# A planner's filler matmuls and the spacing of indirect writes: two of its numbers changed in a fused attention and mixture-of-experts kernel

## The chip, the cores and the metric

The kernel runs on one core of one Trainium2 chip. The metric is device time in microseconds (us), shown as the median of three runs; lower is better. Beside it stands one profiled execution, whose trace is read here. The engines are PE (TensorE matmuls; PEld is its weight load), DVE (VectorE), ACT (ScalarE), POOL (GpSimd) and SP, which issues most DMAs. Every engine works through its own instructions in the order in which they were written.

## The reference

The attention output of 8 batches x 8 heads x 576 tokens x 64 is laid out as 4608 tokens of 512 numbers, and goes through a layer of 8 experts in which each token visits one expert:

```python
scores = scale * np.matmul(q, k.transpose(0, 1, 3, 2))       # window 32; heads 4 to 7 dilated by 4
scores = np.where(masks[None, :, :, :], scores, -1000000000.0)
attn = softmax(scores)                                       # with 1e-9 in the divisor
x = np.matmul(attn, v) -> (4608, 512)
logits = x @ w_gate                                          # (4608, 8)
expert_idx = np.argmax(logits, axis=1)
y[token] = gate_w * (np.maximum(x[token] @ w1[e], 0.0) @ w2[e])   # e = expert_idx[token], F = 1024
```

All of it is float32.

## The kernel before

**The attention** is cut into 32 units: a batch, a kind of mask, and two heads. A unit goes through `turn` (DVE transposes of q and k), `scores` (PE, line 595), `masked` (DVE, line 611), `lowest` (DVE, line 623), `exps` (ACT, line 629), `inverse` (DVE, lines 640 and 642), `norm` (POOL, line 646), `weights` (PE transposes in three groups of three, line 657), an eviction of each group to the tile eT (ACT or DVE, line 878), `summed` (PE, line 676, tile xo), and `put_x` (ACT or DVE, lines 687 and 689). The tile eT has one buffer, `two` (xo, lp and xrow in PSUM) one, and `misc` (the weights in PSUM and others) two.

**The route** of a batch follows its four units: `parts_of_logits` (PE, tile lp), a copy to ls, `logits` (PE, line 976), `choose` and `count` (DVE), `ranks` (PE, lines 1007 and 1010), `places_of` (DVE), `to_rows` (PE transposes, tile xrow, line 939), `rows_out` (ACT or DVE, line 950), and five indirect writes of rows to a table in DRAM, `bucket` (POOL, line 493). After batches 1, 2, 4 and 7, DVE also works out tables of which rows the next slots take.

**The experts** run in 33 slots of 128 rows: a read of rows from `bucket` (SP), a transpose (DVE, line 1407), 32 matmuls of 128x128 into `ph` (line 1415), two evictions, 8 matmuls of 128x512 into `py` (line 1431), an eviction, and an indirect write to the output (POOL, line 1456). Fourteen short blocks of 4 x 32 rows (tiles own, ph_s, py_s) stand between later slots. The last three slots come after the planned part.

**The order** of every engine is made by `Plan.write` while the kernel is being built. Each piece of work is a step with a planned duration, steps that it comes after, buffers that it takes, and a rank. The planner keeps a time at which each engine is free, takes the step with the lowest rank among those that can start soonest, and writes it down. An indirect write on POOL that follows another one is planned no sooner than `APART` after it, and `pass_time` puts `IDLE` memsets of a 128x1 tile, `still`, ahead of it (line 722). `APART` is 0.21 us for each memset.

**The fillers** are matmuls that nobody reads. Until the first expert step is written (`plan.until`), each PE step that is planned to start later than PE is free gets fillers of 0.22 planned us ahead of it (`fill`, line 714): as many whole ones as go into the wait less 0.2 us, at most 12, or two where the planner holds PE's clock to be low. A filler multiplies the tile `idle` by itself into the fourth quarter of the PSUM bank that `weights` (or `ranks`) last took, and so it carries that tile's name: `weights<-idle`, `rank<-idle`, or `unread<-idle` before there is one. It waits for what that bank waits for.

Of the kernel before, what the change touches and what calls it, by code (L numbers as in the profile page):

```python
# [63 lines left out]
STEP_W = 1.0  # L64
ROUTE = 5.0

IDLE = 7

MOVED = 3.0
MOVED_S = 1.5  # L70
# [47 lines left out]
class Plan:  # L118
# [12 lines left out]
    SLACK = 0.2  # L131
    WARM = 0.36
    MOST = 12
    WARMING = 2
    BIAS = 1.5
    COSTS = {"DVE": BIAS}

    APART = 0.21 * IDLE

# [66 lines left out]
    def write(self):  # L206
        left = list(self.steps)
        waiting = {id(s): sum(a.end is None for a in s.after) for s in left}
        needs = {}
        for s in left:  # L210
            for a in s.after:
                needs.setdefault(id(a), []).append(s)
        open_ = [s for s in left if not waiting[id(s)]]
        n = len(left)
        while open_:
            found = []
            for s in open_:
                free = [h.ring.free_at() for h in s.takes]
                if None not in free:
                    found.append(min(  # L220
                        (self.could(s, free, e) for e in s.engines),
                        key=lambda f: f[0] + s.us[f[2]] + self.COSTS.get(f[2], 0.0),
                    ))
            soon = min(f[0] for f in found) + self.SOON
            at, _, e, s = min((f for f in found if f[0] <= soon), key=lambda f: (f[1], f[0]))
            if e == "PE" and self.fill and not self.filled(s):
                idle, cold = at - self.free[e] - self.SLACK, self.slowed(at) > 1.0
                us = self.FILL * self.slowed(self.free[e])
                for _ in range(max(min(self.MOST, int(idle / us)), self.WARMING if cold else 0)):
                    self.fill()  # L230
                    self.free[e] = self.matmuls(self.free[e], self.FILL, self.FILL)
            if e == "PE":
                at = max(at, self.free[e])
                s.end = self.matmuls(at, s.us[e], s.dense, s.slow)
            else:
                s.end = at + s.us[e]
            self.free[e] = s.end
            s.on = None if s.moved else e
            if s.moved and e == "POOL" and self.last_indirect and self.APART:
                self.idle()  # L240
            if e == "POOL":
                self.last_indirect = bool(s.moved)
            if s.moved and e == "POOL":
                if at < self.wrote + self.BURST:
                    if not self.bursts or self.bursts[-1][1] < self.wrote:
                        self.bursts.append((self.wrote, 0.0))
                    self.bursts[-1] = self.bursts[-1][0], s.end + self.AFTER
                self.wrote = s.end
            if s.moved:
                lanes = self.lanes[e == "POOL"]  # L250
                t = s.end - s.dmas * self.ISSUE.get(e, 0.0)
                for _ in range(s.dmas):
                    t = max(t + self.ISSUE.get(e, 0.0), lanes.pop(0))
                    self.moving = max(self.moving, t + 0.65 * self.LANDS) + s.moved / s.dmas
                    lanes.append(self.moving + 0.35 * self.LANDS)
                self.free[e], s.end = t, lanes[-1]
            for h in s.takes:
                h.ring.holds.append(h)
            s.emit(e)
            for h in s.uses:  # L260
                h.left -= 1
                if s.end >= h.end:
                    h.end, h.on = s.end, s.on
            open_.remove(s)
            n -= 1
            for w in needs.get(id(s), ()):
                waiting[id(w)] -= 1
                if not waiting[id(w)]:
                    open_.append(w)
        assert n == 0  # L270
# [58 lines left out]
def kernel(  # L329
# [390 lines left out]
    def pass_time():  # L720
        for _ in range(IDLE):
            nc.gpsimd.memset(still, 0.0)  # L722
# [1115 lines left out]
```

## Time and profile before

| what | us |
|---|---|
| median of 3 runs (780.31 to 782.7) | 781.12 |
| profiled execution | 781.74 |
| span in the trace | 780.0 |
| PE busy in the span | 742.8 |
| DVE, ACT, POOL busy | 257.6, 265.2, 193.5 |

Around the span of the profiled execution lie 1.7 us. A row of the timeline has the start, the duration, the engine, the line, the operation and its tiles as out<-in; in square brackets is the idle time of the engine just before it and what ended that. Here "issue" is idle time in which the engine waited for nothing that the profile shows. A float32 matmul leaves two records on PE, so that x24 of a filler are 12 fillers; a transpose of `weights` or `xrow` leaves one. Neighbouring instructions of one kind are merged into a row.

### The profile page before, as it was taken

Reading aid. Unit: us, or ns where it says so; the run is one execution under the profiler, and the core shown is the slowest. Engines: PE = TensorE matmul, PEld = TensorE weight load, DVE = VectorE, ACT = ScalarE, POOL = GpSimd, SP = SyncE. Lnnn points to the kernel's source line nnn. Section 1 sums busy time; section 2 is a strip of 40 time slices with the busy share of each in tenths; the row PEclk is TensorE's granted clock in tenths of the full one; section 3 lists DMA queues with packets and bytes.
Section 4 is the critical chain, followed back from the end, with each engine's and each line's share of the span. In section 5 each row is a group of like instructions: output and inputs, shape, how many; then the busy total and the mean of one; then the engine's idle time right before and its main releaser. Section 6 shows DMA issues by size and latency. Waiting matters only on the chain.

```text
span 780.0 us, 21889 instructions
## 1 busy us (share of the span) xinstructions
PE 742.8 (95%) x8406; PEld 562.4 (72%) x8406; DVE 257.6 (33%) x718; ACT 265.2 (34%) x868; POOL 193.5 (25%) x641
## 2 busy tenths in 40 slices
PE   5879989999999999999999999999999999999996
PEld 5768878868787776776776776777776776766664
DVE  7958858678857740710000000000000000000000
ACT  2766756576747754211111111111111111111100
POOL 1314343425253434260100100211221111102101
PEclk9989999999999999999999999999999999999999
DMA  9878775969997979799629684727678166099660
GB/s 274 301 224 272 229 239 137 361 190 323 260 268 178 298 226 350 262 387 323 214 47 314 201 258 100 254 51 250 196 261 299 35 226 261 22 316 351 257 222 30
DMA packets 140399, 180.68 MB, mean 232 GB/s; under 512 B 68764, under 2 KB 90014, under 8 KB 139776
## 3 DMA queue, kind: packets, MB, share of 16 engines
q1 hardware_dynamic: 132864, 159.00, 64.1%
q0 software_dynamic: 6272, 19.43, 6.5%
q8 instruction: 68, 1.11, 0.6%
q10 hardware_dynamic: 1152, 0.78, 0.4%
q14 instruction: 43, 0.35, 0.1%
HBM read 252.03 MB, written 19.95 MB: 349 GB/s over the span
## 4 chain that ended last, share of the span: by engine, by line
PE 80%; issue 8%; DMA 6%; DVE 3%; ACT 2%; POOL 1%; SPq 0%; POOLq 0%; DVEq 0%; ACTq 0%
PE ph L1415 27%; PE py L1431 25%; PE scores L595 6%; PE xo L676 6%; PE weights L657 4%; DMA qT<-in_moe_w_dram 4%; PE py_s L1545 3%; PE ph_s L1518 3%; PE weights L714 3%; PE xrow L939 2%; PE lp L962 1%; DMA raw<-in_k_dram 1%; DMA x<-bucket 1%; PE logits L976 1%; ACT eT L878 1%
## 5 line engine op out<-in xcount | busy, mean ns | idle before, releaser
L1415 PEld LDWEIGHTS ph<-xt,w 128*128 128x128 f32 x2112 | 243.2, 192 | 15.7 <-issue 14.6
L1415 PE MATMUL ph<-xt,w 128*128 128x128 f32 x2112 | 252.5, 277 | 0.0
L1431 PE MATMUL py<-w,h 128*128 128x512 f32 x528 | 236.5, 594 | 0.6 <-ACT h L1426 0.6
L1431 PEld LDWEIGHTS py<-w,h 128*128 128x128 f32 x528 | 96.0, 190 | 101.3 <-issue 100.8
L629 ACT ACTIVATE e<-e,lo 128x96 f32<-128x96 f32 x288 | 103.5, 363 | 19.6 <-DVE lo L623 19.6
L1407 DVE STREAM_TRANSPOSE xt<-x 128x512 f32<-128x512 f32 x30 | 21.3, 711 | 243.7 <-PE ph L1415 240.4
L1456 POOL DMA_INDIRECT out_dram<-y,to x30 | 29.5, 984 | 251.7 <-ACT y L1436 249.2
L646 POOL TENSOR_TENSOR e<-e,rec 128x864 f32<-128x864 f32 x32 | 52.3, 1633 | 141.1 <-DVE rec L642 112.6
L1426 ACT ACTIVATE h<-ph 128x512 f32<-128x512 f32 x63 | 37.6, 597 | 142.6 <-PE ph L1415 141.8
L1436 ACT ACTIVATE y<-py,gt 128x512 f32<-128x512 f32 x30 | 20.6, 687 | 157.8 <-PE py L1431 150.3
L595 PE MATMUL scores<-kT,qT 32*64 32x96 f32 (+1 forms) x2160 | 56.2, 259 | 12.0 <-issue 7.4
L595 PEld LDWEIGHTS scores<-kT,qT 32*64 32x64 f32 (+1 forms) x2160 | 49.1, 139 | 18.5 <-issue 14.3
L722 POOL MEMSET still<- 128x1 f32 x504 | 51.4, 102 | 25.0
L629 ACT ACTIVATION_READ_ACCUMULATOR e<-e,lo 128x1 f32 x288 | 54.4, 189 | 0.0
L493 POOL DMA_INDIRECT bucket<-rows,idx x40 | 39.2, 980 | 60.9 <-issue 16.9
L676 PEld LDWEIGHTS xo<-eT,v 96*64 96x64 f32 x1280 | 40.9, 138 | 12.3 <-issue 4.5
L657 PE MATMUL weights<-cst,e 128*96 128x128 f32 x288 | 45.1, 282 | 4.5 <-ACT eT L878 2.1
L611 DVE SCALAR_TENSOR_TENSOR e<-scores,cst 128x384 f32<-128x384 f32 (+1 forms) x128 | 45.5, 395 | 10.0 <-PE scores L595 9.0
L676 PE MATMUL xo<-eT,v 96*64 96x64 f32 (+1 forms) x1280 | 45.9, 225 | 3.0 <-issue 2.6
L878 ACT COPY eT<-weights 96x384 f32<-96x384 f32 x88 | 39.9, 480 | 22.8 <-PE weights L657 16.1
L657 PEld LDWEIGHTS weights<-cst,e 128*96 128x96 f32 x288 | 30.2, 129 | 17.2 <-issue 6.8
L1511 DVE STREAM_TRANSPOSE own<-own 128x128 f32<-128x128 f32 x14 | 4.3, 304 | 99.3 <-DMA own<-bucket 99.3
(168 smaller groups left out, 566.5 us busy)
## 6 DMA issues: line engine op xcount, KB each, us to landing
w<-in_moe_w_dram SPq DMA_DIRECT2D x66, 2048.0 KB
raw<-in_moe_w_dram SPq DMA_DIRECT2D x42, 1024.0 KB
qT<-in_moe_w_dram SPq DMA_DIRECT2D x28, 512.0 KB
w<-in_moe_w_dram SPq DMA_DIRECT2D x8, 1024.0 KB
raw<-in_q_dram SPq DMA_DIRECT2D x14, 576.0 KB
raw<-in_k_dram SPq DMA_DIRECT2D x14, 576.0 KB
x<-bucket SPq DMA_DIRECT2D x120, 64.0 KB
v<-in_v_dram SPq DMA_DIRECT2D x7, 864.0 KB
```

The source lines that it names most:

```text
L493: nc.gpsimd.indirect_dma_start(out=bucket, out_offset=bass.IndirectOffsetOnAxis(ap=idx, axis=0), in_=rows, in_offset=None, bounds_check=NR ...
L595: nc.tensor.matmul(two[r][QB * half : QB * half + QB, KB * c : KB * c + KB], lhsT=qT[:, QB * n : QB * n + QB], rhs=kt[:, QB * n : QB * n + ...
L611: nc.vector.scalar_tensor_tensor(out=e[p, c0 : c0 + w], in0=sc[r][p, a : a + w], scalar=-SCALE, in1=m[p, a : a + w], op0=OP.mult, op1=OP.add,)
L629: nc.scalar.activation(out=ev[:, c], in_=ev[:, c], func=AF.Exp, bias=lo[:, c : c + 1], scale=-1.0, accum_out=den[:, c : c + 1],)
L646: nc.gpsimd.tensor_tensor(out=ev, in0=ev, in1=rec.unsqueeze(2).broadcast_to([128, NC, KB]), op=OP.mult)
L657: nc.tensor.transpose(tp[0:KB, c], ev[:, 3 * g + c], ident)
L676: nc.tensor.matmul(xo[DH * r : DH * r + DH, g, lo - half_s * g : hi - half_s * g], lhsT=v0[:, hd, n] if ty == 0 else v1[:, n, hd], rhs=eT[ ...
L722: nc.gpsimd.memset(still, 0.0)
L878: copier(e)(S_["eT"][:, 3 * g : 3 * g + 3], S_["w", g][0:KB, 0:3])
L1415: nc.tensor.matmul(ph[:, f % 4], lhsT=w1s[j % 2][:, c, 128 * f : 128 * f + 128], rhs=xt[:, c], start=c == 0, stop=c == 3,)
L1426: nc.scalar.activation(to, ph, AF.Relu)
L1431: nc.tensor.matmul(py, lhsT=h[:, f], rhs=w2s[j % 2][:, f], start=f == 0, stop=f == 7)
```

## The change

Two numbers. `IDLE` goes from 7 to 10, so that ten memsets stand between two indirect writes where seven did, and `APART` in the planner follows it (1.47 to 2.1 us). And a wait of PE that is planned to be no longer than 0.9 us beyond the 0.2 us of slack gets no fillers any more, save the two that are written where the planner holds the clock to be low.

```diff
-IDLE = 7
+IDLE = 10
...
+
+    SHORT_WAIT = 0.9
...
-                for _ in range(max(min(self.MOST, int(idle / us)), self.WARMING if cold else 0)):
+                many = min(self.MOST, int(idle / us)) if idle > self.SHORT_WAIT else 0
+                for _ in range(max(many, self.WARMING if cold else 0)):
```

Since the planner counts the fillers and the spacing in its times, the written order moves on every engine. All lines after the second edit stand 3 lines further down. Fillers in the written order go from 133 to 91: 27 stand before the first `weights` in both; from there to the first `logits` 30 become 20, to the second 25 become 10, to the third 41 become 25, and to the first expert matmul 10 become 9. There are 72 groups of memsets in both.

The first place is on PE, from the `ranks` of batch 1 on (its second route). A row is a run of equal instructions; `xo` is `summed`, in three rows a unit. Before:

```order
L714 MATMUL weights<-idle 128x128 x3
L1007 MATMUL rank<-front,idle 128x48
L1010 MATMUL rank<-oh,cst 128x40
L657 MATMUL weights<-cst,e 96x128 x3
L714 MATMUL weights<-idle 128x128 x12
L657 MATMUL weights<-cst,e 96x128 x6
L714 MATMUL weights<-idle 128x128
L676 MATMUL xo<-eT,v_71 64x64 x8
L676 MATMUL xo<-eT,v_71 64x32 x4
L676 MATMUL xo<-eT,v_71 64x64 x8
L657 MATMUL weights<-cst,e 96x128 x3
L714 MATMUL weights<-idle 128x128 x3
```

After, at the same step:

```order
L1010 MATMUL rank<-front,idle 128x48
L1013 MATMUL rank<-oh,cst 128x40
L717 MATMUL rank<-idle 128x128 x6
L942 MATMUL xrow<-cst,xT_74 128x2x2x32 x8
L660 MATMUL weights<-cst,e 96x128 x6
L717 MATMUL weights<-idle 128x128 x4
L942 MATMUL xrow<-cst,xT_74 128x2x2x32 x4
L679 MATMUL xo<-eT,v_71 64x64 x8
L679 MATMUL xo<-eT,v_71 64x32 x4
L679 MATMUL xo<-eT,v_71 64x64 x8
L717 MATMUL weights<-idle 128x128 x4
L660 MATMUL weights<-cst,e 96x128 x3
```

The twelve fillers between the two halves of a unit's transposes are gone, as are the groups of three and the single one; six and four stand at other steps, and the `xrow` transposes of the route now come after `ranks` instead of before.

The second place is on POOL, the five writes of batch 1's route; TENSOR_TENSOR is `norm`. Before:

```order
L493 DMA bucket<-rows,idx 36992x520
L722 MEMSET still 128x1 x7
L493 DMA bucket<-rows,idx 36992x520
L722 MEMSET still 128x1 x7
L493 DMA bucket<-rows,idx 36992x520
L722 MEMSET still 128x1 x7
L493 DMA bucket<-rows,idx 36992x520
L646 TENSOR_TENSOR e<-e,rec 128x864
L493 DMA bucket<-rows,idx 36992x520
```

After:

```order
L496 DMA bucket<-rows,idx 36992x520
L725 MEMSET still 128x1 x10
L496 DMA bucket<-rows,idx 36992x520
L649 TENSOR_TENSOR e<-e,rec 128x864
L496 DMA bucket<-rows,idx 36992x520
L725 MEMSET still 128x1 x10
L496 DMA bucket<-rows,idx 36992x520
L725 MEMSET still 128x1 x10
L496 DMA bucket<-rows,idx 36992x520
```

The `norm` moves from behind the fourth write to behind the second.

The third place is on PE, where the first expert matmuls (`ph`) stand. Before:

```order
L1010 MATMUL rank<-oh,cst 128x40
L676 MATMUL xo<-eT,v_71 64x64 x8
L676 MATMUL xo<-eT,v_71 64x32 x4
L676 MATMUL xo<-eT,v_71 64x64 x8
L714 MATMUL rank<-idle 128x128
L657 MATMUL weights<-cst,e 96x128 x3
L1415 MATMUL ph<-xt,w_0_90 128x128 x8
```

After:

```order
L1013 MATMUL rank<-oh,cst 128x40
L679 MATMUL xo<-eT,v_71 64x64 x8
L679 MATMUL xo<-eT,v_71 64x32 x4
L679 MATMUL xo<-eT,v_71 64x64 x8
L717 MATMUL rank<-idle 128x128 x4
L660 MATMUL weights<-cst,e 96x128 x12
L679 MATMUL xo<-eT,v_71 64x64 x8
L679 MATMUL xo<-eT,v_71 64x32 x4
L679 MATMUL xo<-eT,v_71 64x64 x8
L1418 MATMUL ph<-xt,w_0_90 128x128 x8
```

One more unit's `weights` and `summed` stand ahead of the first expert matmul: 14 `summed` instead of 13, beside 16 units of `scores` in both.

## Rows read from the trace of the kernel before

**Rows 1.** The page's first part: busy us, share of the span and instructions of each engine.

```profile
PE 742.8 (95%) x8406; PEld 562.4 (72%) x8406; DVE 257.6 (33%) x718; ACT 265.2 (34%) x868; POOL 193.5 (25%) x641
```

**Rows 2.** The chain that ended last, as shares of the span, by engine and by line. L714 is the fillers.

```profile
PE 80%; issue 8%; DMA 6%; DVE 3%; ACT 2%; POOL 1%; SPq 0%; POOLq 0%; DVEq 0%; ACTq 0%
PE ph L1415 27%; PE py L1431 25%; PE scores L595 6%; PE xo L676 6%; PE weights L657 4%; DMA qT<-in_moe_w_dram 4%; PE py_s L1545 3%; PE ph_s L1518 3%; PE weights L714 3%; PE xrow L939 2%; PE lp L962 1%; DMA raw<-in_k_dram 1%; DMA x<-bucket 1%; PE logits L976 1%; ACT eT L878 1%
```

**Rows 3.** Stretches of the span: start and end, length, busy us of PE, PEld, DVE, ACT and POOL (with instructions), granted clock of PE as a share of full speed, DMA share, GB/s. The cuts are at the first transposes of a later unit, at the first, second and third `logits`, and at the first expert matmul.

```profile
26.00:61.00 35.00, 29.07 (x640) 25.47 (x640) 25.93 (x52) 24.96 (x107) 7.39 (x5) 0.90 0.84 274
61.00:91.00 30.00, 28.52 (x521) 24.81 (x517) 24.88 (x57) 21.88 (x90) 13.69 (x31) 1.00 0.85 281
91.00:127.00 36.00, 32.70 (x612) 28.77 (x611) 26.09 (x84) 20.07 (x72) 13.18 (x30) 1.00 0.68 211
127.00:136.50 9.50, 8.37 (x98) 7.57 (x96) 7.56 (x28) 7.11 (x25) 3.23 (x7) 1.00 0.42 83
136.50:327.00 190.50, 183.61 (x2661) 145.35 (x2660) 120.43 (x343) 116.44 (x415) 72.12 (x198) 1.00 0.89 273
327.00:733.00 406.00, 402.59 (x3310) 286.32 (x3309) 29.76 (x118) 61.45 (x115) 75.65 (x356) 1.00 0.66 223
```

**Rows 4.** The same stretches for the fillers (L714) alone: PE busy and PEld busy, granted clock, DMA share, GB/s.

```profile
26.00:61.00 35.00, 9.13 (x60) 8.26 (x60) 0.90 0.84 274
61.00:91.00 30.00, 7.09 (x50) 6.28 (x50) 1.00 0.85 281
91.00:127.00 36.00, 11.55 (x84) 9.92 (x82) 1.00 0.68 211
```

**Rows 5.** Timeline of PE, fillers that themselves waited for something first, and the transposes that follow the longest group.

```profile
26.08 0.94 PE L714 MATMUL weights<-idle 128*128 128x128 f32 x6 [0.56 <-ACT eT L878]
...
69.05 0.71 PE L714 MATMUL rank<-idle 128*128 128x128 f32 x4 [0.29 <-DVE pick L1018]
...
98.72 0.94 PE L714 MATMUL weights<-idle 128*128 128x128 f32 x6 [0.66 <-DVE eT L878]
...
100.98 2.94 PE L714 MATMUL weights<-idle 128*128 128x128 f32 x24 [0.62 <-ACT eT L878]
103.77 0.82 PE L657 MATMUL weights<-cst,e 128*96 128x128 f32 x6
...
108.33 0.94 PE L714 MATMUL weights<-idle 128*128 128x128 f32 x6 [0.56 <-ACT eT L878]
```

**Rows 6.** Timeline, short groups of fillers on PE, and the instructions of DVE and ACT that the step behind them needs.

```profile
39.47 1.45 DVE L611 SCALAR_TENSOR_TENSOR e<-scores,cst 128x384 f32<-128x384 f32 x4 [0.43 <-PE weights L657]
...
41.63 0.61 PE L714 MATMUL weights<-idle 128*128 128x128 f32 x4
...
88.46 0.82 DVE L971 COPY ls<-lp 128x640 f32<-128x640 f32 x1 [0.15 <-PE lp L962]
...
89.02 0.83 PE L714 MATMUL weights<-idle 128*128 128x128 f32 x6
...
90.56 0.61 PE L714 MATMUL weights<-idle 128*128 128x128 f32 x4
90.76 1.02 ACT L950 COPY rows<-xrow 128x1024 f32<-128x1024 f32 x1 [0.66 <-PE xrow L939]
...
92.04 0.69 PE L714 MATMUL weights<-idle 128*128 128x128 f32 x4
```

**Rows 7.** Timeline of PE, steps that still waited although fillers stood ahead of them.

```profile
58.08 1.09 PE L939 MATMUL xrow<-cst,xT 128*128 128x128 f32 x8 [0.26 <-DVE ls L971]
...
96.68 1.39 PE L676 MATMUL xo<-eT,v 96*64 96x64 f32 x40 [0.23 <-ACT rows L950]
```

**Rows 8.** Timeline, an eviction on ACT that stands behind a unit's exponentials, and scores on PE that stop in the middle.

```profile
34.41 0.46 ACT L878 COPY eT<-weights 96x384 f32<-96x384 f32 x1
...
47.02 2.55 PE L595 MATMUL scores<-kT,qT 32*64 32x96 f32 x94 [3.95 <-issue]
```

**Rows 9.** Timeline of batch 1's writes: the reciprocal that `norm` needs, a group of memsets, the last write ahead of `norm`, `norm`, and DVE's transposes after its longest wait here.

```profile
105.36 0.22 DVE L642 RECIPROCAL rec<-den 128x9 f32<-128x9 f32 x1
...
107.85 1.06 POOL L722 MEMSET still<- 128x1 f32 x7
...
109.56 0.97 POOL L493 DMA_INDIRECT bucket<-rows,idx  x1 [0.65 <-issue]
...
110.55 1.65 POOL L646 TENSOR_TENSOR e<-e,rec 128x864 f32<-128x864 f32 x1
...
114.26 1.44 DVE L549 STREAM_TRANSPOSE kT<-raw 128x320 f32<-128x320 f32 x2 [6.28 <-PE scores L595]
```

**Rows 10.** Stretches of 3 us, with the columns of rows 3.

```profile
36.00:39.00 3.00, 1.90 (x24) 1.67 (x25) 2.93 (x5) 1.12 (x3) 1.38 (x1) 1.00 1.02 408
42.00:45.00 3.00, 1.07 (x53) 0.76 (x51) 1.84 (x6) 3.00 (x11) 1.27 (x1) 1.00 1.18 204
45.00:48.00 3.00, 0.98 (x48) 0.98 (x53) 0.82 (x1) 3.00 (x18) 0.36 (x1) 0.73 0.75 218
48.00:51.00 3.00, 3.00 (x69) 2.73 (x55) 0.59 (x2) 0.09 (x1) 0.00 (x0) 0.50 0.91 342
51.00:54.00 3.00, 2.96 (x38) 2.62 (x38) 2.92 (x8) 0.00 (x0) 1.04 (x1) 0.63 0.55 202
```

## The prediction

> **What bounds the kernel now.** I read the chain of waits first. 80% of it is PE work, and the two expert lines alone are 52%; no other engine has over 3%. The fillers (L714), which compute nothing, have 3% [rows 2]. PE is busy 742.8 of 780.0 us [rows 1], so the kernel ends when PE has done its fixed work, plus what PE idles, plus what fillers take where real work could have run.
>
> Then the stretches. From 136.5 us, the first expert matmul, to 733 PE is busy 586.2 of 596.5 us at full clock [rows 3]: it always has expert work to put into a gap, and there are no fillers. Before that it has none, and lives on what DVE, ACT and POOL hand it. From 26 to 136.5 us PE is busy 98.7 us of 110.5, of which 9.1 + 7.1 + 11.6 us up to 127 us are fillers (durations overlap a little) [rows 3, 4]. DVE is the busiest of the others with 84.5 us of the same 110.5, ACT has 74.0, POOL 37.5 [rows 3]. So no engine fills this front; it goes at the pace of a loop over engines, and DVE's 26 us of slack are the room there is. Progress gained here is kept: work done before 136.5 us needn't be done later on a full PE.
>
> **The fillers, which go from 133 to 91.** A filler takes 0.22 us: twelve of them lie between 100.98 and the next transposes at 103.77, less the tail of the last record [rows 5]. 42 fewer are 9.2 us of PE time. That is not the gain, since a filler costs nothing while the next step waits. I looked at what the step behind each short group needed.
>
> Some were free: `xrow` at 58.08 still waited 0.26 us for DVE, `summed` at 96.68 still 0.23 us for ACT [rows 7]. Some came late. A filler writes into a bank that an eviction is reading, so it can sit out the wait itself and run when the wait is over. Four groups did that: those at 26.08, 98.72 and 108.33 (three fillers each, behind the eviction) and at 69.05 (two) [rows 5]. The steps behind them, `summed`, `ranks`, `summed` and `weights`, needed the same event or an older one, so each group is pure delay: 3 x 0.66 + 0.44 = 2.42 us. Four more were overtaken: `scores` behind 41.63 had its banks free at 40.92 (39.47 + 1.45), so 0.44 us; `xrow` behind 89.02 could start at 89.28 (88.46 + 0.82), and did at about 89.68, 0.35 us with the handover; `logits` behind 90.56 was open since 89.28, 0.44 us; `xrow` behind 92.04 was open at 91.78 (90.76 + 1.02), so its whole 0.44 us [rows 6]. That is 1.67 us, and 4.1 us for the eight.
>
> The longest group, twelve at 100.98, is no short one, but the new order has none there. It waited 0.62 us for ACT's eviction and then held the unit's remaining transposes until 103.77 [rows 5]: 12 x 0.22 = 2.64 us. What it held up is seen on DVE: 6.28 us idle until scores let it go on at 114.26 [rows 9].
>
> Together 6.7 us. Two of these bought nothing: the group at 26.08 (0.66 us) feeds a loop whose next eviction stands on ACT behind exponentials until 34.41, and the one at 41.63 (0.44 us) stands ahead of a 3.95 us stop of PE in mid-scores, ended by nothing that the profile shows, at 47.02 [rows 8]. I take both off: 5.6 us.
>
> **The spacing, ten memsets for seven.** Seven memsets took 1.06 us [rows 9], so three more are 0.45 us for each gap. The 72 groups make 33 us of POOL time, but POOL is busy only a quarter of the span [rows 1], and after 327 us it has 406 us for 76 us of work [rows 3]; there the gaps are free. In the front they count where `norm` stands behind writes. Batch 1's `norm` had its reciprocal at 105.58 and started at 110.55, behind three gaps and four writes [rows 9]. The new order puts it behind the second write, with one gap. So at batch 1 the longer gap costs 0.45 us and two gaps are saved; at other routes `norm` can stand one or two longer gaps late. From the row its cost lies between -5.0 us (that wait gone, and on the path) and +0.9 us (two gaps on the path). PE was at work while `norm` ran and until the scores of 111.6 had ended, so I stay near the upper end: a loss of 0.6 us.
>
> A rule of the Trainium skill was weighed here ("SBUF — State Buffer", Who interferes with whom): GpSimd shares a port pair with some VectorE instructions, and whoever comes second is blocked for the whole instruction. By it more memsets are more chances to hold DVE. The trace doesn't show that: no wait of DVE in these stretches is ended by a memset. By rule and row the sum stays.
>
> **The order that moves with both.** In the new order one more unit's `weights` and `summed` stand ahead of the first expert matmul, which is how a faster front would look there: not an earlier expert start but more attention done by it. Between 136.5 and 733 us the order moves too; PE idles 6.9 and 3.4 us there [rows 3], and I take no change, 3 us to either side.
>
> **The sum.** -5.6 + 0.6 = -5.0 us. The profiled execution took 781.7 us, so 776.7; it lies 0.6 us above the median, and beside the median I say 776 us. The step I trust least is that lateness on PE is lateness of the front.
>
> **Rivals.**
>
> *Fillers were no bound (no change).* DVE works 84.5 of 110.5 us [rows 3], and the two rows of steps that still waited [rows 7] speak for a front paced by DVE and ACT, in which fewer fillers only turn into idle time. Against it: DVE's 6.28 us wait for scores [rows 9], and 3% of the chain on fillers [rows 2]. It also covers the case that the change misses what is late: 64 fillers remain behind the first `weights`, and those that wait for an eviction go on coming late. Lateness of 6.7 us minus as much new waiting gives 780 to 782.
>
> *More than I count.* If all 42 fillers were in the way, 9.2 us go, and if the 3.95 us stop [rows 8] moves off the path with the other order, 13.2: 768 to 772. For it speaks DVE's slack of 26 us, against it the free groups.
>
> *The clock falls (slower).* PE ran at 1.2 GHz, 0.50 of the full 2.4, from 48 to 51 us, with 0.73 before and 0.63 after; ahead of that PE had been busy 1.07 and 0.98 us in two stretches of 3 us. In 36 to 39 us it was busy 1.90 us and kept 1.00 [rows 10]. The low time cost 0.27 x 0.98 + 0.50 x 3.00 + 0.37 x 2.96 = 2.9 us of work. Without fillers, PE in the two stretches from 61 to 127 us has 21.4 and 21.2 us of work for 30 and 36 us, 2.1 and 1.8 us in 3 [rows 3, 4]. That is above the row that fell and about at the one that held, but an average has thin places, and the new order itself puts in three pairs of warming fillers between the first two `logits`: its planner expects a low clock there. One fall eats 2.9 of the 5.0 us; from two on (5.8 us) the kernel is slower; three give 781.7 - 5.0 + 8.7 = 785.4.
>
> The Trainium skill has a rule that makes this worse ("TensorE: Matmul & The Clock Gate", Part 4: PE-mode transpose): transposes on PE do not count as activity for the clock as matmuls do. Then stretches of `weights` and `xrow`, left without fillers, would count as almost idle. No row here separates transposes from matmuls, since fillers stood among them; that the rule holds is part of this rival's chance.
>
> *The reshuffled order loses.* POOL's longer gaps stand ahead of `norm` at three routes and a fetch of weights or rows comes late on the full PE: 6 gaps x 0.45 us + 3 us on an unchanged front is 787 at worst, 784 as a middle. Nothing in the trace points to it.
>
> **Chances.** Forecast (774 to 778.5) 0.42; more than that 0.13; no change 0.24; the clock 0.12; the order 0.09. About 0.3% (2.3 us) is what a measurement here tells from no change, so faster means under 778.8: 0.42 + 0.13 less a little, 0.54; within it 0.24; slower 0.22. The forecast's own range is 774 to 778.5; the range that should hold the time 8 times in 10 goes from 768.5 (42 fillers and the stop) to 785 (three falls of the clock).
>
> **What would show it.** Right: the first expert matmul at about the same time or a few us earlier, with the extra `summed` before it; PE busy with fillers about 9 us less and its idle time up by less than 5; DVE's share between the second and third `logits` up from 26.1 of 36.0 us, with no 6 us wait for scores; POOL's groups of memsets at 1.5 us; clock 1.00 from 57 us on. Wrong: as many us of new PE waits as fillers went (the front is DVE's), a granted clock under 1 between 61 and 136 us, or a gain or loss that lies behind 136.5 us, where I expect none.

## The result and the profile after

The changed kernel is slower: 787.05 us (median of 20 runs, 780.65 to 790.87) against 783.44 us (20 runs, 775.57 to 793.25) beside it; ratio 1.0052, 95% interval 1.0034 to 1.0071. Run once more beside other kernels (e19 below) it came to 1.0029 [1.0003, 1.0055]. The forecast was 776.7 us where the profiled execution before took 781.7 (0.994), 776 beside its median, and the range ended at 785.

The execution profiled after took 790.9 us with a span of 789.1, so it lies 3.8 us above its median; what it lost is larger than what the median lost. Single executions of one kernel lie 10 us and more apart here, so the ratios carry the verdicts and the traces the places. A ratio leaves out runs over 1.5% above the fastest of their kernel: three of twelve for e3, e12 and e18, two for e6 and e16, one for e15, and one to three of the 29 to 35 of the kernel before beside them; for e3, e12 and e18 the median of all runs is given too.

The page: busy times and the chain by line, which answer to [rows 1, 2], and the group of the memsets.

```profile
PE 746.0 (95%) x8322; PEld 563.3 (71%) x8322; DVE 258.0 (33%) x714; ACT 266.1 (34%) x872; POOL 214.4 (27%) x857
...
PE ph L1418 27%; PE py L1434 25%; PE scores L598 6%; PE xo L679 4%; PE weights L660 4%; PE py_s L1548 3%; PE ph_s L1521 3%; DMA qT<-in_moe_w_dram 2%; PE xrow L942 2%; PE weights L717 2%; PE lp L965 1%; DMA x<-bucket 1%; ACT e L632 1%; PE logits L979 1%; DVE e L614 1%
...
L725 POOL MEMSET still<- 128x1 f32 x720 | 72.5, 101 | 37.5
```

PE is busy 3.2 us longer than in [rows 1], with 42 fillers less. The fillers alone (line 714 before, 717 after), over the whole span: PE busy, PEld busy, granted clock, DMA share, GB/s. Of the kernel before:

```profile
0.00:780.00 780.00, 39.78 (x266) 35.54 (x266) 0.99 0.72 232
```

Of the kernel after:

```profile
0.00:789.10 789.10, 29.88 (x182) 27.30 (x182) 0.97 0.71 229
```

So 9.9 us of fillers went. PE's idle time is the span less its busy time: 780.0 - 742.8 = 37.2 before, 789.1 - 746.0 = 43.1 after. What is left of the busy time, PE's own work, went from 742.8 - 39.8 = 703.0 to 746.0 - 29.9 = 716.1 us: the same matmuls took 13.1 us longer. -9.9 + 5.9 + 13.1 = 9.1, the difference of the two spans.

The stretches of [rows 3] after (the first expert matmul is now at 142.1):

```profile
26.00:61.00 35.00, 27.23 (x629) 23.04 (x624) 27.03 (x53) 25.08 (x107) 8.48 (x6) 0.95 0.88 278
61.00:91.00 30.00, 26.82 (x413) 22.58 (x412) 19.02 (x47) 18.94 (x71) 11.98 (x38) 0.83 0.71 235
91.00:127.00 36.00, 32.60 (x566) 28.57 (x565) 26.68 (x85) 22.78 (x88) 14.42 (x39) 0.86 0.70 231
127.00:142.10 15.10, 13.66 (x226) 11.97 (x223) 12.61 (x43) 9.23 (x34) 6.37 (x15) 1.00 0.40 91
142.10:327.00 184.90, 174.52 (x2555) 138.37 (x2553) 110.45 (x285) 111.88 (x408) 75.50 (x249) 0.97 0.88 266
327.00:733.00 406.00, 404.95 (x3255) 289.06 (x3254) 39.53 (x164) 63.35 (x117) 87.08 (x482) 1.00 0.65 221
```

The granted clock, third column from the right, says where: 0.83 and 0.86 between 61 and 127 us, where [rows 3] have 1.00. In stretches of 3 us:

```profile
57.00:60.00 3.00, 2.83 (x81) 2.55 (x81) 2.92 (x9) 3.00 (x11) 0.00 (x0) 1.00 0.48 109
60.00:63.00 3.00, 3.00 (x22) 2.98 (x21) 1.98 (x8) 2.05 (x12) 1.63 (x1) 0.72 0.88 235
63.00:66.00 3.00, 2.29 (x16) 1.59 (x16) 2.80 (x9) 2.07 (x10) 0.46 (x1) 0.71 1.05 417
69.00:72.00 3.00, 3.00 (x38) 2.59 (x40) 2.88 (x9) 0.47 (x1) 1.94 (x11) 0.50 0.38 149
72.00:75.00 3.00, 3.00 (x25) 2.85 (x22) 0.93 (x1) 1.11 (x2) 1.88 (x11) 0.50 0.29 68
96.00:99.00 3.00, 3.00 (x17) 2.98 (x17) 1.57 (x9) 2.18 (x13) 0.00 (x0) 0.52 1.04 375
114.00:117.00 3.00, 2.97 (x51) 2.74 (x51) 1.56 (x3) 2.81 (x16) 1.58 (x1) 0.50 0.62 245
```

Four falls, from about 61, 69, 96 and 113 us. (The profiled execution of e19, the same kernel, has a span of 778.1 us, and in these stretches two falls, from about 94 and 114 us.) The part of full speed that was missing, times PE's busy time, summed over all stretches of 3 us from 57 to 123, is 9.5 us. What it does to one piece of work is seen on PE's timeline: `summed` (40 records) at half clock and, 7 us later, at full clock; and, past the front, the longest new wait.

```profile
70.32 2.40 PE L679 MATMUL xo<-eT,v 96*64 96x64 f32 x40
...
77.26 1.39 PE L679 MATMUL xo<-eT,v 96*64 96x64 f32 x40
...
177.53 1.11 PE L942 MATMUL xrow<-cst,xT 128*128 128x128 f32 x4 [5.77 <-DVE rows L953]
```

PE waits 5.77 us there for a copy of batch 3's rows. On DVE's timeline that copy stands behind an expert block's transpose, which waits for batch 2's bucket:

```profile
173.28 0.71 DVE L1410 STREAM_TRANSPOSE xt<-x 128x512 f32<-128x512 f32 x1 [6.85 <-DMA x<-bucket]
...
176.24 1.23 DVE L953 COPY rows<-xrow 128x1024 f32<-128x1024 f32 x1
```

Batch 1's writes on POOL, which answer to [rows 9]: ten memsets take 1.52 us, and `norm` starts 6 us earlier, without a wait.

```profile
101.23 1.52 POOL L725 MEMSET still<- 128x1 f32 x10
...
104.40 1.65 POOL L649 TENSOR_TENSOR e<-e,rec 128x864 f32<-128x864 f32 x1
```

### The profile page after: what moved, and what is told of

It reads as the page before. It is cut to its first block, busy times and chain, and to the rows that moved or that the text cites. A ratio compares the mean times of both kernels' runs of the same rounds, so it can differ in the third digit from the quotient of the medians.

```text
span 789.1 us, 21922 instructions
## 1 busy us (share of the span) xinstructions
PE 746.0 (95%) x8322; PEld 563.3 (71%) x8322; DVE 258.0 (33%) x714; ACT 266.1 (34%) x872; POOL 214.4 (27%) x857
## 4 chain that ended last, share of the span: by engine, by line
PE 79%; issue 8%; DVE 4%; DMA 3%; POOL 2%; ACT 1%; SPq 1%; POOLq 0%; DVEq 0%; ACTq 0%
PE ph L1418 27%; PE py L1434 25%; PE scores L598 6%; PE xo L679 4%; PE weights L660 4%; PE py_s L1548 3%; PE ph_s L1521 3%; DMA qT<-in_moe_w_dram 2%; PE xrow L942 2%; PE weights L717 2%; PE lp L965 1%; DMA x<-bucket 1%; ACT e L632 1%; PE logits L979 1%; DVE e L614 1%
## 5 line engine op out<-in xcount | busy, mean ns | idle before, releaser
L725 POOL MEMSET still<- 128x1 f32 x720 | 72.5, 101 | 37.5
L598 PE MATMUL scores<-kT,qT 32*64 32x96 f32 (+1 forms) x2160 | 59.2, 263 | 13.6 <-issue 8.3
L598 PEld LDWEIGHTS scores<-kT,qT 32*64 32x64 f32 (+1 forms) x2160 | 51.2, 142 | 20.3 <-issue 16.1
L679 PE MATMUL xo<-eT,v 96*64 96x64 f32 (+1 forms) x1280 | 47.6, 228 | 4.4 <-issue 2.9
L660 PE MATMUL weights<-cst,e 128*96 128x128 f32 x288 | 47.9, 294 | 2.3 <-ACT eT L881 0.9
L881 ACT COPY eT<-weights 96x384 f32<-96x384 f32 x93 | 41.6, 479 | 21.2 <-PE weights L660 17.4
L660 PEld LDWEIGHTS weights<-cst,e 128*96 128x96 f32 x288 | 32.6, 136 | 15.4 <-issue 6.6
L626 DVE TENSOR_REDUCE lo<-e 128x9 f32<-128x864 f32 x32 | 33.1, 1033 | 0.7
```

The lines of the kernel that those rows point to most:

```text
L598: nc.tensor.matmul(two[r][QB * half : QB * half + QB, KB * c : KB * c + KB], lhsT=qT[:, QB * n : QB * n + QB], rhs=kt[:, QB * n : QB * n + ...
L660: nc.tensor.transpose(tp[0:KB, c], ev[:, 3 * g + c], ident)
L679: nc.tensor.matmul(xo[DH * r : DH * r + DH, g, lo - half_s * g : hi - half_s * g], lhsT=v0[:, hd, n] if ty == 0 else v1[:, n, hd], rhs=eT[ ...
L881: copier(e)(S_["eT"][:, 3 * g : 3 * g + 3], S_["w", g][0:KB, 0:3])
```

## The experiments

Three things changed at once: fillers, memsets, and the order that the planner makes of both. Three theories: the clock (too few fillers), the spacing (late writes, late bucket reads), and the order by itself. Lines of the diffs are from the kernel named. No run leaves out any of the computation. Times and clocks are medians of 12 runs (e2: 6); the clock is the mean granted over the span, and of the kernel before it had medians from 0.986 to 0.988 beside them.

### Parts of the change, planned anew: e1, e2

e1, the kernel before with the spacing alone:

```diff
-IDLE = 7
+IDLE = 10
```

> The spacing alone: ten memsets between indirect writes in place of seven, short waits still filled, the order planned anew for that (135 fillers). Clock theory: the fillers are there, so the granted clock stays at 1.00 from 57 us on as in the kernel before, and the time is within 2 us of it. Spacing theory (the longer gaps push batch 2's writes and the first bucket reads late, so that PE waits some 6 us near 177 us): this kernel alone shows most of the loss, 3 to 5 us slower, with the clock at 1.00. Order theory (any newly planned order loses): slower by 2 to 5 us with no single place for it.

782.0 us, 1.0014 [0.9979, 1.0050], clock 0.985. No loss that can be told, although PE waited 6.19 us for rows near 175 us in this order too. So a newly planned order need not lose, and a wait there need not show in the time.

e2, the changed kernel with `IDLE = 7`: the short waits alone.

> The short waits alone: waits of at most 0.9 us get no fillers, seven memsets as before, the order planned anew for that (79 fillers). Clock theory: the granted clock falls at two or more places between 57 and 127 us, PE loses 6 to 10 us of work there, and the time is 2 to 6 us above the kernel before. Spacing theory: the memsets are as before, so the forecast's gain is seen, 3 to 6 us faster. Order theory: open, since the order is a third one; the clock stays at 1.00.

791.2 us, 1.0123 [1.0079, 1.0167], clock 0.9645: the worst of all. The clock falls as its theory has it, but the loss is beyond the 6 us that I gave it, and PE idles 10.4 us between 90 and 126 us (before: 3.3). Each of these kernels has an order of its own, so the next runs hold the order fixed.

### The order held, one thing changed: e3, e4, e5, e7, e10, e18, e19

e3: the planner counts the fillers of short waits, but they are not written.

```diff
-                for _ in range(max(min(self.MOST, int(idle / us)), self.WARMING if cold else 0)):
-                    self.fill()
+                least = self.WARMING if cold else 0
+                many = min(self.MOST, int(idle / us))
+                kept = max(many if idle > self.SHORT_WAIT else 0, least)
+                for i in range(max(many, least)):
+                    if i < kept:
+                        self.fill()
```

> The order of the kernel before, kept instruction for instruction, less the fillers of waits of at most 0.9 us (93 of 133 are left): nothing but fillers differs. Clock theory: the granted clock falls between 57 and 127 us, and the 4 us of lateness that go are eaten by 6 us or more of low clock: 1 to 6 us slower. Spacing and order theories: neither the memsets nor the order changed, so the clock stays at 1.00 and 2 to 5 us are gained.

0.9973 [0.9939, 1.0008]; all runs 780.6 beside 780.4; clock 0.9725. The page's busy times of its profile, and its fillers over the whole span:

```profile
PE 744.0 (96%) x8326; PEld 563.2 (72%) x8326; DVE 257.4 (33%) x718; ACT 265.3 (34%) x868; POOL 193.5 (25%) x641
```

```profile
0.00:779.00 779.00, 30.11 (x186) 28.08 (x186) 0.97 0.71 232
```

9.7 us of fillers less, own work 744.0 - 30.1 = 713.9 us, 10.9 more, PE's idle time 2.2 less, and a span 1.0 us shorter. Fillers and clock cancel: the clock theory is right about the clock, and wrong that it decides.

e5 is the reverse: the changed kernel's order, fillers written into its short waits but not counted.

```diff
-                for _ in range(max(many, self.WARMING if cold else 0)):
+                least = self.WARMING if cold else 0
+                full = max(min(self.MOST, int(idle / us)), least)
+                for i in range(full):
                     self.fill()
-                    self.free[e] = self.matmuls(self.free[e], self.FILL, self.FILL)
+                    if i < max(many, least):
+                        self.free[e] = self.matmuls(self.free[e], self.FILL, self.FILL)
```

> The order and the ten memsets of the changed kernel, kept instruction for instruction, with fillers put back into its waits of at most 0.9 us (129 fillers): nothing but fillers differs from the changed kernel. Clock theory: the granted clock is back at 1.00 from 57 us on and the loss is gone: within 2 us of the kernel before, or up to 3 us faster. Spacing and order theories: as slow as the changed kernel or 3 us slower than that, since the fillers come late again: 4 to 7 us above the kernel before.

783.8 us, 1.0050 [1.0018, 1.0081], clock 0.985 where the kernel before has 0.987. The clock is back but for that, and the loss is as it was.

e4, the order of before with ten memsets (`IDLE = 10`, and `APART = 0.21 * 7` so that the planner still counts seven):

> The order of the kernel before, instruction for instruction, with ten memsets in each gap in place of seven: the spacing without a new order. Spacing theory: the longer gaps themselves delay writes and fetches, 3 to 5 us slower, with new waits of DVE or PE for batch 2's rows near 177 us. Order theory: within 2 us of the kernel before. In both the clock stays at 1.00 after 57 us.

779.6 us, 0.9984 [0.9959, 1.0009]. Batch 2's five writes took 1.9 us more, as they must (four gaps of 0.45), and nothing came of it.

e7, the changed kernel with seven memsets and the planner still counting ten:

> The changed kernel's order and fillers, with seven memsets in each gap in place of ten. Spacing theory: the loss of the changed kernel that is not the clock's goes, 4 us or more faster than it, so about the time of the kernel before. Order theory: as slow as the changed kernel, 3 to 5 us above the kernel before, with the wait of PE for the rows copy near 177 us still there. In both the clock is low between 60 and 120 us as in the changed kernel.

781.9 us, 1.0017 [0.9984, 1.0050], clock 0.9735, the wait for rows still 5.47 us. Between the two expectations, so a run with the fillers back had to tell: e10 is e5 with seven memsets, so that only the order differs from the kernel before, and with it the places and the number of the fillers (129 for 133).

> The changed kernel's order with fillers put back into its short waits, and seven memsets in each gap in place of ten: against the kernel before only the order of the steps differs. If the loss is the order's (a copy of rows on DVE behind a transpose that waits for a bucket, so that PE waits near 175 us), the time is still 3 to 4 us above the kernel before, with a wait of PE for rows of 3 us or more. If it is the longer gaps' (batch 2's five writes take 1.9 us more and everything that reads that bucket is later), the wait shrinks by 2 us and the time is within 2 us of the kernel before.

788.4 us, 1.0071 [1.0035, 1.0108], wait for rows 5.45 us. The order loses by itself. Part of that goes with the clock: its median is 0.983 where the kernel before has 0.988. At an equal clock, 0.985 to 0.991, five executions of e10 took 785.7 us on average and 25 of the kernel before 783.7, 2 us less. For e5 the same sorting leaves 3 us (7 executions at 782.4, 19 at 779.3).

Last, e18 is e3 with e4's edit, the old order with both other parts of the change, and e19 the changed kernel beside it.

> The order of the kernel before with both other parts of the change: no fillers in its short waits, ten memsets in each gap. If the order is the whole loss and the other two parts are worth what they measured alone (0.9973 and 0.9984), 0.994 to 0.999 of the kernel before at a clock of 0.970 to 0.976. If the parts lose together what they don't lose alone, 1.003 or more.

> The changed kernel again, unchanged, beside the three others: 1.003 to 1.007 of the kernel before, its clock 0.962 to 0.983. By the order theory it is 5 us or more slower than e18; by a loss of the parts together it is the same.

e18: 0.9977 [0.9944, 1.0009], all runs 780.5 beside 780.35, clock 0.9765. e19: 783.15 us, 1.0029 [1.0003, 1.0055], clock 0.9735. All eight together, as ratios to the kernel before:

| | fillers in short waits, 7 memsets | the same, 10 memsets | none, 7 memsets | none, 10 memsets |
|---|---|---|---|---|
| order of before | 1 | 0.9984 | 0.9973 | 0.9977 |
| order of after | 1.0071 | 1.0050 | 1.0017 | 1.0029 and 1.0052 |

Along each column the order costs: 0.7%, about 5 us, in the two left ones (0.6% by the medians of all runs), and 0.4 to 0.75% in the two right ones (0.1 to 0.4% by the medians of all runs). The third column alone isn't clear of noise. Ten memsets in place of seven make -0.2 to +0.35%, with no steady sign. Fillers out of the short waits make -0.5 to 0.0%: a small gain at most.

### The place where the order was thought to lose: e12, e16, e17

e12, the changed kernel with batch 3's copies of rows on ACT alone:

```diff
-                    ("ACT", "DVE"), us, lambda e, g=g: rows_out(e, g), after=[pe],
+                    ("ACT",) if b == 3 else ("ACT", "DVE"), us, lambda e, g=g: rows_out(e, g), after=[pe],
```

> The changed kernel, with the copies of batch 3's rows left to ACT alone, so that none of them stands on DVE behind the expert's transpose that waits for its bucket; the order behind that place is planned anew. If that is where the order loses, PE's wait of 5.8 us near 177 us falls to 2 or 3 us and the time is 2 to 4 us below the changed kernel, about 1.001 to 1.003 of the kernel before. If the wait only moves to the next step that needs DVE, the time stays at 1.004 to 1.006.

0.9981 [0.9946, 1.0017]; the median of all its runs is 784.8 beside 783.4. PE's wait moved on: 6.09 us for `choose`, which stands on DVE behind the same transpose. Inconclusive in time, clear as to the wait: it is DVE that is blocked, not the copy alone. So e16 moves the transpose itself.

```diff
         pl = add("DVE", 0.6, lambda e: places_of(), after=[rk], uses=[hb], rank=rank + 0.3)
+        if b == 3:
+            chosen.append(pl)
...
-            xt = add("DVE", 0.72, lambda e, j=j, D=D: D.update(xt=across(j)), after=[xl],
+            xt = add("DVE", 0.72, lambda e, j=j, D=D: D.update(xt=across(j)),
+                     after=[xl, *(chosen if j == READY[1] else ())],
```

> The changed kernel with one step of DVE put later: the transpose of the first expert block that reads batch 2's bucket waits in the plan until batch 3's places are known, so it stands behind that batch's copy of rows; the order behind it is planned anew. If the order loses where that transpose blocks DVE, PE's wait of 5.8 us near 177 us goes and the time is 3 to 5 us below the changed kernel. If PE waits there because it has nothing else to do until the bucket is read, the wait comes back a few us later at the expert's first matmul and the time stays within 1.5 us of the changed kernel.

782.5 us, 1.0032 [1.0002, 1.0061], the same as e19. The wait is gone, and another has come. PE in the changed kernel (e19):

```profile
174.85 1.12 PE L942 MATMUL xrow<-cst,xT 128*128 128x128 f32 x4 [5.68 <-DVE rows L953]
```

PE in e16, the same transposes, and two expert steps much later:

```profile
170.24 0.60 PE L943 MATMUL xrow<-cst,xT 128*128 128x128 f32 x4
...
349.49 8.80 PE L1437 MATMUL py<-w,h 128*128 128x512 f32 x16 [2.76 <-DMA w<-in_moe_w_dram]
362.61 3.84 PE L1421 MATMUL ph<-xt,w 128*128 128x128 f32 x32 [0.75 <-ACT h L1432]
```

In the 65 us from the first expert matmul on PE idles 0.6 us where e19 has 6.4, and 3.5 us are waited out at 349 and 363 us instead, for weights and an eviction. Neither expectation saw that: the wait comes back, though not at the expert's first matmul.

e17 is the same edit in e5.

> The same step put later in the copy of the changed kernel whose short waits have their fillers back. That copy was 1.005 of the kernel before at an equal clock, with a wait of 3.7 us near 174 us. If the blocked DVE is the order's loss, 0.998 to 1.002; if not, 1.003 to 1.007.

781.3 us, 1.0031 [1.0002, 1.0060]: not told apart from e5, and with the same new waits (2.73 and 0.75 us).

### The late fillers, and what holds the clock: e9, e11, e15, e6

e9 tests the prediction's own list. Fillers are numbered as they are written; the eight short groups and the twelve are left out, and nothing else moves.

```diff
+    sizes = {27: 3, 45: 2, 64: 2, 77: 3, 80: 2, 82: 2, 86: 3, 89: 12, 105: 3}
+    dropped = {f + i for f, n in sizes.items() for i in range(n)}
+    nth = [0]
+
     def fill():
-        nc.tensor.matmul(spare[0], lhsT=idle, rhs=idle, start=True, stop=True)
+        nth[0] += 1
+        if nth[0] - 1 not in dropped:
+            nc.tensor.matmul(spare[0], lhsT=idle, rhs=idle, start=True, stop=True)
```

> The order of the kernel before, less the 32 fillers that the prediction found late: its eight short groups (20 fillers) and the group of twelve; the other 101 stay. By the prediction's sum 5 to 6.7 us faster with the clock at 1.00 from 57 us on. Clock theory: the granted clock falls once or twice between 61 and 127 us and takes 3 to 9 us of it back, so between 2 us slower and 3 us faster. If lateness of PE is not lateness of the front, PE idles 5 us more and the time is the same at a clock of 1.00.

778.1 us, 0.9950 [0.9921, 0.9980]: faster than both kernels. PE's timeline, the transposes that the twelve had held, and the first expert matmul; then the third stretch:

```profile
98.68 0.83 PE L657 MATMUL weights<-cst,e 128*96 128x128 f32 x6 [1.40 <-DVE cnt L1148]
...
131.88 1.95 PE L1421 MATMUL ph<-xt,w 128*128 128x128 f32 x16
```

```profile
91.00:127.00 36.00, 33.45 (x595) 29.47 (x594) 28.07 (x91) 23.24 (x89) 12.17 (x30) 0.91 0.70 217
```

The first expert matmul comes 4.6 us earlier (136.51 before). One fall in this stretch, from 99 us on, is in the way, in the place of the twelve; two more follow it, from about 168 and 195 us; the clock's median is 0.9805.

e11 is e9 with the twelve back.

> The order of the kernel before, less the 20 fillers of the eight short groups alone; the group of twelve stays. By the prediction's working 3 to 4 us come off the front: the first expert matmul at 132.5 to 133.5 us, the clock 1.00 from 57 us to there, and 2 to 4 us faster in all. If the run with 32 fillers out owes its gain to the group of twelve, the first expert matmul stays within 1.5 us of 136.5 and the time within 1.5 us of the kernel before.

780.7 us beside 783.4, 0.9966 [0.9936, 0.9995], clock 0.987, first expert matmul at 134.7: the eight short groups are worth 2.7 us by the ratio, with an interval from 0.4 to 5.0.

e15 is e9 with five of the twelve back (`94: 7` in place of `89: 12`) and twelve fillers at a wait of PE near 168 us:

```diff
     def weights(ev, g):
+        made[0] += 1
+        if made[0] == 52:
+            for _ in range(12):
+                nc.tensor.matmul(spare[0], lhsT=idle, rhs=idle, start=True, stop=True)
```

> The kernel with 32 late fillers out, mended at its two falls of the clock: five of the group of twelve are back (1.1 us, where PE waited 1.4 us), and twelve fillers stand ahead of the transposes near 167.8 us, where PE waited 3.6 us. If the falls are what holds that kernel back, the clock is 1.00 from 57 us on, some 3 to 6 us more are gained, and the time is 0.987 to 0.992 of the kernel before. If the low clock near 168 us lies where PE waits for data anyway, it stays at 0.993 to 0.996.

778.0 us beside 783.4, 0.9940 [0.9913, 0.9967], clock 0.985, first expert matmul at 135.8. The falls are mended, and 0.1% more than e9 is nothing that can be told. That the low clock lay where PE waits anyway fits this; no run shows it by itself.

e6 replaces the fillers' matmul.

```diff
-        nc.tensor.matmul(spare[0], lhsT=idle, rhs=idle, start=True, stop=True)
+        for _ in range(2):
+            nc.tensor.transpose(spare[0], idle, ident)
```

> The order of the kernel before, each filler now two transposes on PE where it was one matmul; both are unread. If transposes hold the clock as matmuls do, it stays at 1.00 from 57 us on and the time is within 3 us of the kernel before, less or more by how long two transposes last beside the 0.22 us of a filler. If they don't, as the Trainium skill has it (TensorE: Matmul & The Clock Gate, Part 4: PE-mode transpose), the clock falls at least as far as in the run without the short-wait fillers, PE's work takes 10 us longer and the time is 5 us or more above the kernel before.

1.0001 [0.9964, 1.0038], clock 0.9865. The third stretch, and the fillers in it:

```profile
91.00:127.00 36.00, 33.04 (x624) 28.91 (x623) 27.08 (x87) 20.95 (x75) 13.31 (x30) 1.00 0.69 214
```

```profile
91.00:127.00 36.00, 11.66 (x88) 9.54 (x86) 1.00 0.69 214
```

With transposes for fillers the clock is 1.00 there, as in [rows 3] with matmuls. So the rule that the prediction took from the Trainium skill ("TensorE: Matmul & The Clock Gate", Part 4: PE-mode transpose), that transposes don't count for the clock as matmuls do, is not what this kernel shows. Whether transposes with no matmuls among them would raise the clock, no run here shows.

## Why the prediction was wrong, step by step

**The order, "I take no change, 3 us to either side": this step turned the sign.** It was put at nothing, and it costs about 5 us where it differs and memsets and short-wait fillers don't (e10 against before, e5 against e4). Against the kernel before, 2 us (e10) and 3 us (e5) stay at an equal clock; the rest of e10's loss goes with the lower clock of its runs. I had argued that nothing in the trace points to it and gave it 0.09.

The trace did show one candidate. In the new order the rows copy stands on DVE behind a transpose that waits for a bucket; in the old one ACT has it, and only `choose` stands behind that transpose (1.76 us of waiting). Both orders could be read beforehand, and of the order the prediction read PE and POOL only. A row each of PE's busy time in the 65 us from the first expert matmul on, with the granted clock, DMA share and GB/s: before, e5 and e10.

```profile
136.51:201.51 65.00, 61.20 (x1125) 1.00 0.90 283
...
140.25:205.25 65.00, 59.25 (x1069) 1.00 0.90 279
...
147.24:212.24 65.00, 58.26 (x978) 0.95 0.89 281
```

PE idles 3.8 us in the profile of before, 5.8 in e5's and 6.7 in e10's, and the low clock there takes 2.9 us more in e10. But two kernels that didn't lose speak against it as the cause. The same stretch of e1 and of e3, which has the old order:

```profile
139.79:204.79 65.00, 57.38 (x1001) 0.95 0.90 279
...
137.17:202.17 65.00, 58.85 (x1009) 0.95 0.93 289
```

PE idles 7.6 and 6.2 us there, more than in e5, at a lower clock, and neither kernel can be told from the one before. And with that wait gone in e16 and e17, waits for weights and an eviction come 180 us later, and their ratios, 1.003, are not told apart from those with it. That this order loses is shown; where it loses stays open, since each mend also plans the tail anew.

**The fillers, "133 to 91", 9.2 us of PE time, of which 5.6 late: the clock was left out of this term.** The time that went was 9.9 us. That late ones were late holds: e11's 20 fillers gave 2.7 us by the ratio, against 4.1 on my list, or 3.0 with the two that bought nothing taken off; e9's 32 gave 0.5%, 3.9 us [1.6, 6.2], against 5.6, which lies inside that interval. e9's fall of the clock at 99 us may be the difference, but e15, which mends it, gained no more that can be told. The step that failed is that the change takes out those fillers and leaves the clock alone. It takes out others too: in e3, the old order less 40 fillers of short waits, 9.7 us of fillers went, PE's own work took 10.9 us longer, and the time fell by 2 us by the ratio [-4.8, +0.6] or not at all by the medians of all runs.

**The clock, a rival at 0.12, "one fall 2.9 us".** It happened. In the profiled execution four falls cost 9.5 us in the front, and every kernel without short-wait fillers has a median clock of 0.9645 to 0.977, against 0.983 to 0.988 with them. The size of one fall was fair; the weighing was not: I compared PE's busy time in 3 us, 2.1 and 1.8, with rows that fell at 1.07 and held at 1.90. After, the clock fell behind a stretch with 2.83 of 3 us busy. Busy time in these traces doesn't tell whether the clock holds. Yet taking the fillers out is not what made the kernel slower, since they gave back about as much as the clock took (e3 beside the kernel before, e5 beside the changed one).

**The sum in its own terms.** Fillers with the clock: -5.6 said, -2 to 0 measured (e3). Spacing: +0.6 said, -1 measured (e4), not told from nothing. Order: 0 said, about +5 measured. That makes +2 to +4; the change measured +4.1 us by the ratio [2.7, 5.6].

**"Lateness on PE is lateness of the front", the step I trusted least, held.** With the order kept, e9 and e11 are faster, and in their profiled executions the first expert matmul comes 4.6 and 1.8 us earlier (e15's 0.7). In the changed kernel it comes at 142.1, 5.6 us later (139.3 in e19's), with one more unit's `summed` ahead of it.

**The spacing, +0.6 us between -5.0 and +0.9.** Groups of 1.52 us as worked out, `norm` early; between e4 and the kernel before it costs nothing that can be told. Waits of DVE that the profile puts down to the memsets, 2.2 and 3.4 us, are new; e4 with ten memsets in the old order has none, and e7 and e10 with seven in the new one have 1.8 and 3.4 us, so they come with the new order. Nor do the memsets make DVE's instructions longer: its busy time is 257.8 us in e4 and 257.6 before.

**What would show it.** Fillers 9.9 us less (said 9); idle time up 5.9 (said under 5); DVE's share in the third stretch 26.7 of 36 us, where 26.1 was to rise; its longest wait there 2.2 us, so the 6 us wait did go; clock not 1.00. Of the signs that I had named for being wrong, two came: a granted clock under 1 between 61 and 136 us, and a loss behind 136.5 (PE idles 10.4 us from 142.1 to 327 at a clock of 0.97, where it idled 6.9 at 1.00 [rows 3]).

## What to carry to other kernels

When a planner's number changes, the order is a part of the change: hold it fixed and change the rest. A step that now stands behind a wait for a DMA is a candidate and not yet a cause: here the same wait stood in a kernel with no loss that could be told (e1), and taking it away gained nothing that could be told. Filler work that keeps PE's clock up and filler work that delays PE can be the same instructions; pick the late ones by the timeline (which waited, and what was ready behind them), not by the planned length of a wait: 32 so chosen gave 0.5%, 40 chosen by their planned wait nothing that could be told.

## What was not expected of the hardware

The clock can fall while the profile shows PE without a gap. In e10's profiled execution, with short-wait fillers in place, PE was busy 3.00 of every 3 us from 84 to 93 us and the clock fell, and it fell again at 113; that execution lies 6 us above its median.

```profile
84.00:87.00 3.00, 3.00 (x42) 1.86 (x44) 2.95 (x7) 2.29 (x5) 0.94 (x2) 1.00 0.66 164
87.00:90.00 3.00, 3.00 (x84) 2.88 (x75) 2.97 (x6) 3.00 (x17) 0.00 (x0) 1.00 0.40 88
90.00:93.00 3.00, 3.00 (x82) 2.86 (x82) 2.14 (x13) 1.90 (x6) 0.00 (x0) 0.94 0.64 140
93.00:96.00 3.00, 2.71 (x14) 2.56 (x13) 1.83 (x5) 1.87 (x11) 1.63 (x1) 0.50 0.86 277
```

Other executions of the same kernel had mean clocks up to 0.990 against its 0.974 here. Where the clock falls differs from run to run of one program: the profiled executions of the changed kernel and of e19, the same kernel, fell at different places. And within a kernel the longer runs are mostly those with the lower clock: e10 took 783.5 us at 0.990 and 794.6 at 0.974.
